# Block-wide loads of q, k and v, the weights issued together behind the first block, and the first attention as one chain

## The chip, the cores and the metric

The kernel runs on one core of one Trainium2 chip. The metric is the device time of one execution in microseconds (us); lower is better. TensorE is called PE, VectorE DVE, ScalarE ACT, GpSimd POOL and SyncE SP. SP does nothing here but issue transfers. The stage numbers below count position blocks of 128 from 0 to 5, and batches from 0 to 3.

## The reference

A decaying linear attention (4 batches, 8 heads, 768 positions, head size 64, all fp32) is followed by a two-layer network with a leaky activation on 3072 tokens of width 512:

```python
for b in range(nb):                      # blocks of 64 positions
    intra = einsum('bhic,bhjc->bhij', qb, kb) * Dmask     # lam ** (i - j), lower triangle
    intra = einsum('bhij,bhjd->bhid', intra, vb)
    inter = einsum('bhid,bhde->bhie', qb * lam_pow, kv_state)
    out[:, :, sl] = intra + inter
    kv_state = lam_block * kv_state + einsum('bhsd,bhse->bhde', kb * rev_pow, vb)
x = out.transpose(0, 2, 1, 3).reshape(B * S, H * D)
h = x @ w_in                             # 512 -> 2048
g = maximum(h, 0) + alpha * minimum(h, 0)
return g @ w_out                         # 2048 -> 512
```

## The kernel before

The kernel uses blocks of 128 positions (`L`), six of them (`NSB`), instead of the reference's 64. For each block `sb` and each batch `b` the attention has these steps:

- `load` brings q, k and v, each as a tile of 128 positions by 512 values in fp32 (256 KB). In memory a head's row is 64 values, so every piece of a transfer is 256 bytes. SP issues the loads.
- `casts` turns them into fp16 (`q16`, `k16`, `v16`) and makes `kdec`, the decayed k, on POOL. A string such as "AGG" says which engine casts q, k and v (A is ACT, V is DVE, G is POOL).
- `transposes` turns q16 and k16 on PE and copies them out of PSUM into `qkT`; from block 1 on POOL also makes `qdT`, the decayed q.
- `scores` multiplies k by q on PE; DVE multiplies by `dmask` into `sm`.
- `outputs` adds the state's part (`R` with `qdT`, from block 1 on) and the block's own part (`v16` with `sm`) in the PSUM tile `ot`; ACT copies it into `xT`, which holds all four batches of one block.
- `states` updates `R` with the product of `kdec` and `v16`.

The network follows block by block. `up(c, f)` makes one of 16 slices of 128 hidden units for block `c`: four matmuls into `h_ps`, a Relu of the negative part on ACT (`m`), and one DVE instruction that adds it with the factor `oma` = 1 - alpha. The arguments `b0, nb` restrict it to some batches, so that it can start when half of `xT` is there. `down(c, t, part, nparts)` makes a part of the second product for one batch of the block, and `store` writes it.

The weights come in four quarters each (`load_win`, `load_wout`), issued by POOL, which casts them to fp16 on the way (1 MB read, 512 KB written). All transfers, whoever issues them, run on the same 16 DMA engines.

The order is written out by hand: each engine runs its instructions in the order of the program, and waits only for the data and the buffers that it needs. Lines 399 to 483 are this order for blocks 0 and 1; from line 484 on `weave` alternates the attention steps of a block with `down` and `up` calls, and PE takes them strictly in turn. Two `gate` transfers (2 bytes each) on SP's queue hold back the loads behind them until a quarter of a weight has landed: gate 0 reads a column of `w_in_sb` ahead of block 1's loads, gate 1 a row of `w_out_sb` ahead of block 2's.

With `raw_pool` of six buffers for each of q, k and v, one and a half blocks of loads can be in flight. The attention of block 2 starts with two batches at once:

```python
        steps = [
            lambda: (casts(sb, 0, "AGG"), casts(sb, 1, "AGG")),
            lambda: transposes(sb, 0, "V"),
            lambda: scores(sb, 0),
        ]
```

Of the kernel before, what the change touches and what calls it, by code (L numbers as in the profile page):

```python
# [11 lines left out]
def kernel(  # L12
# [11 lines left out]
    nc = tc.nc  # L24
    ctx.enter_context(tc.manual_schedule())
    fp32 = mybir.dt.float32
# [3 lines left out]
    ALU = mybir.AluOpType  # L30

    B, H, S, D = q.shape
    assert (B, H, S, D) == (4, 8, 768, 64)
    L = 128
    NSB = S // L
    NHP = H // 2
    DM = H * D
    DFF = moe_w_in.shape[1]
    NF = DFF // 128
# [1 line left out]
    CH = B * L  # L41

    const = ctx.enter_context(tc.tile_pool(name="const", bufs=1))
    raw_pool = ctx.enter_context(tc.tile_pool(name="raw", bufs=6))
    half_pool = ctx.enter_context(tc.tile_pool(name="half", bufs=3))
    qkt_pool = ctx.enter_context(tc.tile_pool(name="qkt", bufs=2))
    sm_pool = ctx.enter_context(tc.tile_pool(name="sm", bufs=2))
# [12 lines left out]
    )  # L60
    raws = {}

    def load(sb, b):
        raws[sb, b] = []
        for n, src in zip("qkv", (q, k, v)):
            t = raw_pool.tile([128, DM], fp32, tag=f"{n}raw", name=f"{n}raw")
            nc.sync.dma_start(  # L67
                out=t.rearrange("p (h d) -> p h d", h=H),
                in_=src[b, :, ds(sb * L, L), :].rearrange("h s d -> s h d"),
            )  # L70
            raws[sb, b].append(t)

    w_in_sb = const.tile([128, NHP, DFF], fp16, name="w_in_sb")
    w_out_sb = const.tile([128, NF, DM], fp16, name="w_out_sb")
# [1 line left out]
    def load_win(i):  # L76
        nc.gpsimd.dma_start(
            out=w_in_sb[:, :, ts(i, 512)],
            in_=moe_w_in[:, ts(i, 512)].rearrange("(g p) f -> p g f", p=128),
        )  # L80

    def load_wout(i):
        nc.gpsimd.dma_start(
            out=w_out_sb[:, ts(i, 4), :],
            in_=moe_w_out[ts(i, 512), :].rearrange("(f p) d -> p f d", p=128),
        )
# [3 lines left out]
    def gate(i, w):  # L90

        nc.sync.dma_start(out=gates[:, i : i + 1], in_=w)

    load(0, 0)
    alpha_sb = const.tile([128, NF], fp32, name="alpha_sb")
    load(0, 1)
    nc.sync.dma_start(out=alpha_sb, in_=moe_alpha.rearrange("(t p) -> p t", p=128))
    load(0, 2)
    load(0, 3)


    one = const.tile([128, 1], fp32, name="one")
# [2 lines left out]
    nc.scalar.activation(warm, one, AF.Ln)  # L105
    ident = const.tile([128, 128], fp16, name="ident")
    make_identity(nc, ident)

    rel_i = const.tile([128, L], int32, name="rel_i")
    nc.gpsimd.iota(rel_i, pattern=[[1, L]], base=0, channel_multiplier=-1)  # L110
# [17 lines left out]

    dmask = const.tile([128, 2, NHP, L], fp32, name="dmask")
    for hl in range(2):  # L130
        nc.vector.tensor_tensor(
            out=dmask[:, hl],
            in0=rel_f.unsqueeze(1).to_broadcast([128, NHP, L]),
            in1=llv[:, hl, :].unsqueeze(2).to_broadcast([128, NHP, L]),
            op=ALU.mult,
        )
        nc.scalar.activation(dmask[:, hl], dmask[:, hl], AF.Exp)
        nc.gpsimd.affine_select(
            out=dmask[:, hl],
            in_=dmask[:, hl],  # L140
            compare_op=ALU.is_ge,
            fill=0.0,
            base=0,
            pattern=[[0, NHP], [1, L]],
            channel_multiplier=-1,
        )
# [10 lines left out]
    def late_constants():  # L157
        nc.vector.tensor_tensor(
            out=qdecay,
            in0=pos_f.unsqueeze(1).to_broadcast([128, NHP, L]),  # L160
            in1=llp.unsqueeze(2).to_broadcast([128, NHP, L]),
            op=ALU.mult,
        )
        nc.scalar.activation(qdecay, qdecay, AF.Exp)
        nc.scalar.activation(rdecay, llp, AF.Exp, scale=float(L))
        nc.vector.tensor_scalar(
            out=oma, in0=alpha_sb, scalar1=-1.0, scalar2=1.0, op0=ALU.mult, op1=ALU.add
        )


# [12 lines left out]
            nc.gpsimd.tensor_copy(out=out, in_=in_)  # L183

    def casts(sb, b, eng):
        qr, kr, vr = raws.pop((sb, b))
        q16 = half_pool.tile([128, DM], fp16, tag="q16", name="q16")
        k16 = half_pool.tile([128, DM], fp16, tag="k16", name="k16")
        v16 = half_pool.tile([128, DM], fp16, tag="v16", name="v16")
        copy_on(eng[0], q16, qr)  # L190
        copy_on(eng[1], k16, kr)
        copy_on(eng[2], v16, vr)
        T[sb, b] = dict(q16=q16, k16=k16, v16=v16)
        if sb < NSB - 1:
            kdec = half_pool.tile([128, DM], fp16, tag="kdec", name="kdec")
            nc.gpsimd.tensor_tensor(  # L196
                out=kdec.rearrange("p (h d) -> p h d", h=H),
                in0=kr.rearrange("p (h d) -> p h d", h=H),
                in1=kdecay.unsqueeze(2).to_broadcast([128, H, D]),
                op=ALU.mult,  # L200
            )
            T[sb, b]["kdec"] = kdec
# [194 lines left out]


    casts(0, 0, "VVG")
    load_win(0)  # L400
    transposes(0, 0, "V")
    casts(0, 1, "AAG")
    load_win(1)
    scores(0, 0)
    transposes(0, 1, "V")
    outputs(0, 0)
    scores(0, 1)
    casts(0, 2, "AVG")
    load_win(2)
    states(0, 0)  # L410
    transposes(0, 2, "A")
    outputs(0, 1)
    late_constants()
    scores(0, 2)
    states(0, 1)
    up(0, 0, 0, 2)
    casts(0, 3, "AVG")
    load_win(3)
    up(0, 1, 0, 2)
    outputs(0, 2)  # L420
    up(0, 2, 0, 2)
    transposes(0, 3, "A")
    up(0, 3, 0, 2)
    scores(0, 3)
    states(0, 2)
    outputs(0, 3)
    states(0, 3)
    for f in range(4):
        up(0, f, 2, 2)


    gate(0, w_in_sb[0:1, 0, 1024:1025])
    for b in range(B):
        load(1, b)
    for f in range(4, 11):
        up(0, f)
    casts(1, 0, "AGG")
    transposes(1, 0, "A")
    up(0, 11)
    casts(1, 1, "AGG")  # L440
    scores(1, 0)
    up(0, 12)
    transposes(1, 1, "A")
    up(0, 13)
    outputs(1, 0)
    casts(1, 2, "AGG")
    scores(1, 1)
    up(0, 14)
    states(1, 0)
    load_wout(0)  # L450
    transposes(1, 2, "A")
    up(0, 15)
    outputs(1, 1)
    casts(1, 3, "AGG")
    load_wout(1)
    scores(1, 2)
    up(1, 0, 0, 2)
    up(1, 1, 0, 2)
    states(1, 1)
    transposes(1, 3, "A")  # L460
    up(1, 2, 0, 2)
    outputs(1, 2)
    up(1, 3, 0, 2)
    load_wout(2)
    load_wout(3)
    scores(1, 3)
    up(1, 4, 0, 2)
    up(1, 5, 0, 2)
    states(1, 2)
    up(1, 6, 0, 2)  # L470
    outputs(1, 3)
    up(1, 7, 0, 2)
    states(1, 3)
    for f in range(8):
        up(1, f, 2, 2)
    gate(1, w_out_sb[0:1, 8, 0:1])
    for b in range(B):
        load(2, b)
    for f in range(8, NF):
        up(1, f)  # L480

    for b in range(B):
        load(3, b)
    weave(attention_steps(2), [lambda x=x: down(0, x // 4, x % 4, 4) for x in range(16)])
    for c in range(2, NSB):
        att = []
        if c + 2 < NSB:
            for b in range(B):
                load(c + 2, b)
        if c + 1 < NSB:  # L490
            att = attention_steps(c + 1)
        moe = []
        for f in range(NF):
            moe.append(lambda f=f: up(c, f))
            moe.append(lambda f=f: down(c - 1, f // 4, f % 4, 4))
        weave(att, moe)
# [32 lines left out]
```

## Time and profile before

| what | value |
|---|---|
| median of 3 runs | 247.33 us (245.26 to 249.1) |
| the profiled execution | 246.46 us |
| its span, first to last instruction | 244.7 us |
| PE busy | 217.8 us, 89% of the span |
| DVE, ACT, POOL busy | 124.7, 112.4, 86.3 us |
| DMA, mean over the span | 121 GB/s |
| granted PE clock | 1.00 |

The profile is of one execution. "Busy" adds up the instructions of an engine, whether they lie on the path that sets the end or not; a wait is put down to the instruction or transfer that ended it. "Landing" is the time from the issue of a transfer to its completion as the waiting engine sees it. The time of the profiled execution is 1.76 us longer than its span, for what lies around the first and the last instruction.

### The profile page before, as it was taken

What the parts mean: (1) busy time and instruction counts of PE and PEld (TensorE: products, weight loads), DVE (VectorE), ACT (ScalarE), POOL (GpSimd) and SP (SyncE); (2) the same over time, 40 slices, a digit from 0 to 9 for tenths busy, and PEclk for the clock granted to TensorE, in tenths of its full rate; (3) what the DMA queues carried; (4) which work ended last, traced back from release to release, by engine and by line L of the source; (5) the groups of instructions that cost most, each with busy time, mean ns of one, the idle gap of its engine ahead of it and who ended that gap; (6) DMA issues with size and microseconds to landing.
All of it is one profiled execution on the core that took longest, in us unless ns stands there. A gap on an engine that the chain in (4) does not pass through costs nothing.

```text
span 244.7 us, 4422 instructions
## 1 busy us (share of the span) xinstructions
PE 217.8 (89%) x1728; PEld 110.9 (45%) x1728; DVE 124.7 (51%) x205; ACT 112.4 (46%) x200; POOL 86.3 (35%) x119
## 2 busy tenths in 40 slices
PE   0529597989997998999999999999999999999994
PEld 0316443556443444444444444444444444444453
DVE  3534476768862334566456565556565534444100
ACT  4427667856642324534434535435534443444211
POOL 1823317992058684515641614611330100000000
PEclk9999999999999999999999999999999999999999
DMA  6999699799999999999304901101101100111122
GB/s 140 153 218 196 101 229 218 130 133 183 187 203 246 248 226 260 197 255 220 96 2 119 228 3 43 43 3 43 43 3 43 46 24 20 43 43 46 43 86 86
DMA packets 84936, 29.65 MB, mean 121 GB/s; under 512 B 77620, under 2 KB 81972, under 8 KB 84916
## 3 DMA queue, kind: packets, MB, share of 16 engines
q1 hardware_dynamic: 76948, 18.89, 41.5%
q0 software_dynamic: 4224, 4.19, 11.3%
q10 hardware_dynamic: 3744, 6.30, 7.1%
q8 instruction: 13, 0.21, 0.4%
q14 instruction: 7, 0.06, 0.1%
HBM read 27.28 MB, written 6.29 MB: 137 GB/s over the span
## 4 chain that ended last, share of the span: by engine, by line
PE 67%; DMA 11%; POOL 8%; SPq 5%; ACT 3%; issue 3%; DVE 1%; ACTq 0%; POOLq 0%
PE o_ps L332 27%; PE h_ps L305 25%; DMA vraw<-in_v_dram 9%; PE o_ps L355 6%; SPq L67 5%; DMA w_in_sb<-in_moe_w_in_dram 2%; POOL kdec L196 2%; PE ot L245 2%; PE ot L255 2%; PE s L225 2%; POOL qdT L216 2%; POOL v L183 1%; ACT o_sb L345 1%; PE tp L210 1%; PE kv L283 1%
## 5 line engine op out<-in xcount | busy, mean ns | idle before, releaser
L317 DVE SCALAR_TENSOR_TENSOR g<-m,oma,h_ps 128x512 f16<-128x512 f32 (+1 forms) x108 | 73.6, 687 | 73.0 <-ACT m L314 71.4
L305 PE MATMUL h_ps<-xT,w_in_sb 128*128 128x512 f16 (+1 forms) x432 | 98.0, 359 | 2.8 <-ACT xT L265 1.8
L314 ACT ACTIVATE m<-h_ps 128x512 f32<-128x512 f32 (+1 forms) x108 | 59.4, 550 | 76.2 <-PE h_ps L305 75.4
L332 PE MATMUL o_ps<-w_out_sb,g 128*128 128x512 f16 x320 | 82.2, 380 | 0.4 <-ACT o_sb L345 0.2
L305 PEld LDWEIGHTS <-w_in_sb 128*128 128x128 f16 x432 | 40.1, 99 | 39.3 <-issue 3.6
L216 POOL TENSOR_TENSOR qdT<-qkT,qdecay 128x512 f16<-128x512 f16 x20 | 23.2, 1164 | 67.0 <-DVE qkT L181 65.2
L332 PEld LDWEIGHTS <-g 128*128 128x128 f16 x320 | 28.8, 98 | 32.5 <-issue 0.8
L235 DVE TENSOR_TENSOR sm<-s,dmask 128x512 f16<-128x512 f32 x48 | 30.8, 684 | 12.9 <-PE s L225 12.9
L345 ACT ACTIVATE o_sb<-o_ps 128x512 f32<-128x512 f32 (+1 forms) x25 | 14.5, 580 | 26.6 <-PE o_ps L332 15.5
L208 PE MATMUL tp<-ident,k 128*128 128x128 f16 x96 | 10.0, 230 | 13.5 <-DVE k L181 12.0
L196 POOL TENSOR_TENSOR kdec<-kraw,kdecay 128x512 f16<-128x512 f32 x20 | 20.8, 1042 | 0.0
L265 ACT ACTIVATE xT<-ot 128x512 f16<-128x512 f32 x24 | 14.3, 597 | 13.9 <-PE ot L255 12.8
L183 POOL CAST v<-vraw 128x512 f16<-128x512 f32 x24 | 14.7, 614 | 14.3 <-DMA vraw<-in_v_dram 12.5
L183 POOL CAST k<-kraw 128x512 f16<-128x512 f32 x20 | 12.2, 611 | 18.1 <-DMA kraw<-in_k_dram 18.1
L208 PEld LDWEIGHTS <-k 128*128 128x128 f16 x96 | 7.2, 102 | 18.9 <-DVE k L181 12.1
L179 ACT ACTIVATE q<-qraw 128x512 f16<-128x512 f32 x23 | 14.0, 623 | 1.8 <-DMA qraw<-in_q_dram 1.8
L181 DVE COPY qkT<-tp 128x1024 f16<-128x1024 f16 x18 | 12.4, 690 | 4.5 <-PE tp L210 4.4
L355 PE MATMUL o_ps<-w_out_sb,g 128*128 128x512 f16 (+1 forms) x80 | 14.0, 336 | 0.0
L225 PE MATMUL s<-qkT 64*128 64x128 f16 x192 | 10.2, 229 | 2.5 <-ACT qkT L179 1.5
L255 PE MATMUL ot<-sm,v 128*64 128x128 f16 x192 | 10.8, 236 | 1.1 <-DVE sm L235 1.1
L210 PE MATMUL tp<-ident,q 128*128 128x128 f16 x96 | 10.1, 231 | 1.8 <-ACT q L179 1.6
L225 PEld LDWEIGHTS <-qkT 64*128 64x128 f16 x192 | 5.8, 98 | 11.2 <-issue 6.4
(44 smaller groups left out, 90.0 us busy)
## 6 DMA issues: line engine op xcount, KB each, us to landing
qraw<-in_q_dram SPq DMA_DIRECT2D x24, 256.0 KB, 5.2
kraw<-in_k_dram SPq DMA_DIRECT2D x24, 256.0 KB, 5.2
vraw<-in_v_dram SPq DMA_DIRECT2D x24, 256.0 KB, 5.1
out_dram<-o_sb ACTq DMA_DIRECT2D x23, 256.0 KB, 2.0
w_in_sb<-in_moe_w_in_dram POOLq DMA_DIRECT2D x4, 512.0 KB, 6.3
w_out_sb<-in_moe_w_out_dram POOLq DMA_DIRECT2D x4, 512.0 KB, 7.2
out_dram<-o_sb ACTq DMA_DIRECT2D x2, 128.0 KB, 1.7
lam_sb<-in_lam_dram ACTq DMA_DIRECT2D x1, 4.0 KB, 3.5
```

The source lines that it names most:

```text
L183: nc.gpsimd.tensor_copy(out=out, in_=in_)
L196: nc.gpsimd.tensor_tensor(out=kdec.rearrange("p (h d) -> p h d", h=H), in0=kr.rearrange("p (h d) -> p h d", h=H), in1=kdecay.unsqueeze(2). ...
L208: nc.tensor.transpose(tp[:, 1, hp, :], t["k16"][:, ts(hp, D2)], ident)
L216: nc.gpsimd.tensor_tensor(out=qdT, in0=qkT[:, 0], in1=qdecay, op=ALU.mult)
L225: nc.tensor.matmul(s[hl][:, hp, :], lhsT=t["qkT"][p, 1, hp, :], rhs=t["qkT"][p, 0, hp, :], start=True, stop=True,)
L235: nc.vector.tensor_tensor(out=sm, in0=s[hl], in1=dmask[:, hl], op=ALU.mult)
L305: nc.tensor.matmul(h_ps[:, 0:n], lhsT=w_in_sb[:, gi, ts(f, 128)], rhs=XT[c][:, gi, cols], start=(gi == 0), stop=(gi == NHP - 1),)
L314: nc.scalar.activation(m[:, 0:n], h_ps[:, 0:n], AF.Relu, scale=-1.0)
L317: nc.vector.scalar_tensor_tensor(out=G[c, f][:, cols], in0=m[:, 0:n], scalar=oma[:, f : f + 1], in1=h_ps[:, 0:n], op0=ALU.mult, op1=ALU.add,)
L332: nc.tensor.matmul(o_ps, lhsT=G[c, f][:, ts(t, 128)], rhs=w_out_sb[:, f, :], start=(f == 0), stop=(f == NF - 1),)
L345: nc.scalar.activation(o_sb[:, 0:n], o_ps[:, 0:n], AF.Copy)
L355: nc.tensor.matmul(o_ps[:, 0:n], lhsT=G[c, f][:, ts(t, 128)], rhs=w_out_sb[:, f, ts(x, n)], start=(f == 0), stop=(f == NF - 1),)
```

## The change

- A raw tile now holds all four batches of a block for one of q, k, v (1 MB), with two buffers instead of six of a quarter of that size. Block 0 is loaded as before, one batch at a time into its part of the tile; block 1 in two halves of two batches; blocks 2 to 5 with one transfer for each of q, k and v.
- Alpha is loaded as 16 rows of 128 values at the end of block 0's loads, and turned on PE into a PSUM tile that shares the buffer of `ot`; before, it came column-wise in the middle of these loads.
- The two multiplications of `dmask` move from DVE to POOL, and the two masks that follow on POOL stand behind both.
- All four quarters of w_in are issued by POOL behind the casts of batch 2 of block 0; before, one stood behind each batch's casts. Quarters 1 to 3 of w_out are issued together behind the casts of batch 3 of block 1.
- The attention of block 0 runs through without `up` calls between its steps; `late_constants` moves to its end. The `up` calls of block 0 then cover all four batches at once, eight of them ahead of block 1's first casts.
- Gate 0 reads a column of w_in's second quarter instead of its third. Gate 1 and block 2's loads keep their place in SP's queue.
- The halves of `up(1, 0)` to `up(1, 7)` for batches 2 and 3 stand behind `up(1, 8)` to `up(1, 15)`.

```diff
--- before.py
+++ after.py
@@ -41,7 +41,7 @@
     CH = B * L
 
     const = ctx.enter_context(tc.tile_pool(name="const", bufs=1))
-    raw_pool = ctx.enter_context(tc.tile_pool(name="raw", bufs=6))
+    raw_pool = ctx.enter_context(tc.tile_pool(name="raw", bufs=2))
     half_pool = ctx.enter_context(tc.tile_pool(name="half", bufs=3))
     qkt_pool = ctx.enter_context(tc.tile_pool(name="qkt", bufs=2))
     sm_pool = ctx.enter_context(tc.tile_pool(name="sm", bufs=2))
@@ -60,15 +60,16 @@
     )
     raws = {}
 
-    def load(sb, b):
-        raws[sb, b] = []
-        for n, src in zip("qkv", (q, k, v)):
-            t = raw_pool.tile([128, DM], fp32, tag=f"{n}raw", name=f"{n}raw")
+    def load(sb, b0=0, nb=B):
+        if b0 == 0:
+            raws[sb] = [
+                raw_pool.tile([128, B, DM], fp32, tag=f"{n}raw", name=f"{n}raw") for n in "qkv"
+            ]
+        for t, src in zip(raws[sb], (q, k, v)):
             nc.sync.dma_start(
-                out=t.rearrange("p (h d) -> p h d", h=H),
-                in_=src[b, :, ds(sb * L, L), :].rearrange("h s d -> s h d"),
+                out=t[:, ds(b0, nb), :].rearrange("p b (h d) -> p (b h) d", h=H),
+                in_=src[ds(b0, nb), :, ds(sb * L, L), :].rearrange("b h s d -> s (b h) d"),
             )
-            raws[sb, b].append(t)
 
     w_in_sb = const.tile([128, NHP, DFF], fp16, name="w_in_sb")
     w_out_sb = const.tile([128, NF, DM], fp16, name="w_out_sb")
@@ -91,12 +92,10 @@
 
         nc.sync.dma_start(out=gates[:, i : i + 1], in_=w)
 
-    load(0, 0)
-    alpha_sb = const.tile([128, NF], fp32, name="alpha_sb")
-    load(0, 1)
-    nc.sync.dma_start(out=alpha_sb, in_=moe_alpha.rearrange("(t p) -> p t", p=128))
-    load(0, 2)
-    load(0, 3)
+    for b in range(B):
+        load(0, b, 1)
+    alpha_t = const.tile([NF, 128], fp32, name="alpha_t")
+    nc.sync.dma_start(out=alpha_t, in_=moe_alpha.rearrange("(t p) -> t p", p=128))
 
 
     one = const.tile([128, 1], fp32, name="one")
@@ -105,6 +104,8 @@
     nc.scalar.activation(warm, one, AF.Ln)
     ident = const.tile([128, 128], fp16, name="ident")
     make_identity(nc, ident)
+    ident_f = const.tile([NF, NF], fp32, name="ident_f")
+    nc.vector.tensor_copy(out=ident_f, in_=ident[0:NF, 0:NF])
 
     rel_i = const.tile([128, L], int32, name="rel_i")
     nc.gpsimd.iota(rel_i, pattern=[[1, L]], base=0, channel_multiplier=-1)
@@ -128,13 +129,14 @@
 
     dmask = const.tile([128, 2, NHP, L], fp32, name="dmask")
     for hl in range(2):
-        nc.vector.tensor_tensor(
+        nc.gpsimd.tensor_tensor(
             out=dmask[:, hl],
             in0=rel_f.unsqueeze(1).to_broadcast([128, NHP, L]),
             in1=llv[:, hl, :].unsqueeze(2).to_broadcast([128, NHP, L]),
             op=ALU.mult,
         )
         nc.scalar.activation(dmask[:, hl], dmask[:, hl], AF.Exp)
+    for hl in range(2):
         nc.gpsimd.affine_select(
             out=dmask[:, hl],
             in_=dmask[:, hl],
@@ -163,8 +165,10 @@
         )
         nc.scalar.activation(qdecay, qdecay, AF.Exp)
         nc.scalar.activation(rdecay, llp, AF.Exp, scale=float(L))
+        al = ps.tile([128, NF], fp32, tag="ot", name="al")
+        nc.tensor.transpose(al, alpha_t, ident_f)
         nc.vector.tensor_scalar(
-            out=oma, in0=alpha_sb, scalar1=-1.0, scalar2=1.0, op0=ALU.mult, op1=ALU.add
+            out=oma, in0=al, scalar1=-1.0, scalar2=1.0, op0=ALU.mult, op1=ALU.add
         )
 
 
@@ -183,7 +187,7 @@
             nc.gpsimd.tensor_copy(out=out, in_=in_)
 
     def casts(sb, b, eng):
-        qr, kr, vr = raws.pop((sb, b))
+        qr, kr, vr = (t[:, b, :] for t in raws[sb])
         q16 = half_pool.tile([128, DM], fp16, tag="q16", name="q16")
         k16 = half_pool.tile([128, DM], fp16, tag="k16", name="k16")
         v16 = half_pool.tile([128, DM], fp16, tag="v16", name="v16")
@@ -397,96 +401,87 @@
 
 
     casts(0, 0, "VVG")
-    load_win(0)
     transposes(0, 0, "V")
     casts(0, 1, "AAG")
-    load_win(1)
     scores(0, 0)
     transposes(0, 1, "V")
     outputs(0, 0)
+    casts(0, 2, "AVG")
+    for i in range(4):
+        load_win(i)
     scores(0, 1)
-    casts(0, 2, "AVG")
-    load_win(2)
     states(0, 0)
     transposes(0, 2, "A")
     outputs(0, 1)
-    late_constants()
+    casts(0, 3, "AVG")
     scores(0, 2)
     states(0, 1)
-    up(0, 0, 0, 2)
-    casts(0, 3, "AVG")
-    load_win(3)
-    up(0, 1, 0, 2)
+    transposes(0, 3, "A")
     outputs(0, 2)
-    up(0, 2, 0, 2)
-    transposes(0, 3, "A")
-    up(0, 3, 0, 2)
     scores(0, 3)
     states(0, 2)
+    late_constants()
     outputs(0, 3)
     states(0, 3)
-    for f in range(4):
-        up(0, f, 2, 2)
-
-
-    gate(0, w_in_sb[0:1, 0, 1024:1025])
-    for b in range(B):
-        load(1, b)
-    for f in range(4, 11):
+
+
+    gate(0, w_in_sb[0:1, 0, 512:513])
+    load(1, 0, 2)
+    load(1, 2, 2)
+    for f in range(8):
         up(0, f)
     casts(1, 0, "AGG")
     transposes(1, 0, "A")
+    up(0, 8)
+    scores(1, 0)
+    up(0, 9)
+    casts(1, 1, "AGG")
+    up(0, 10)
+    outputs(1, 0)
     up(0, 11)
-    casts(1, 1, "AGG")
-    scores(1, 0)
+    transposes(1, 1, "A")
+    states(1, 0)
     up(0, 12)
-    transposes(1, 1, "A")
+    scores(1, 1)
+    casts(1, 2, "AGG")
     up(0, 13)
-    outputs(1, 0)
-    casts(1, 2, "AGG")
-    scores(1, 1)
+    load_wout(0)
     up(0, 14)
-    states(1, 0)
-    load_wout(0)
+    outputs(1, 1)
+    up(0, 15)
     transposes(1, 2, "A")
-    up(0, 15)
-    outputs(1, 1)
+    states(1, 1)
+    up(1, 0, 0, 2)
     casts(1, 3, "AGG")
-    load_wout(1)
+    for i in range(1, 4):
+        load_wout(i)
+    up(1, 1, 0, 2)
     scores(1, 2)
-    up(1, 0, 0, 2)
-    up(1, 1, 0, 2)
-    states(1, 1)
+    up(1, 2, 0, 2)
+    up(1, 3, 0, 2)
+    outputs(1, 2)
     transposes(1, 3, "A")
-    up(1, 2, 0, 2)
-    outputs(1, 2)
-    up(1, 3, 0, 2)
-    load_wout(2)
-    load_wout(3)
+    up(1, 4, 0, 2)
+    states(1, 2)
+    up(1, 5, 0, 2)
     scores(1, 3)
-    up(1, 4, 0, 2)
-    up(1, 5, 0, 2)
-    states(1, 2)
     up(1, 6, 0, 2)
+    up(1, 7, 0, 2)
     outputs(1, 3)
-    up(1, 7, 0, 2)
     states(1, 3)
+    for f in range(8, NF):
+        up(1, f)
+    gate(1, w_out_sb[0:1, 8, 0:1])
+    load(2)
     for f in range(8):
         up(1, f, 2, 2)
-    gate(1, w_out_sb[0:1, 8, 0:1])
-    for b in range(B):
-        load(2, b)
-    for f in range(8, NF):
-        up(1, f)
-
-    for b in range(B):
-        load(3, b)
+
+    load(3)
     weave(attention_steps(2), [lambda x=x: down(0, x // 4, x % 4, 4) for x in range(16)])
     for c in range(2, NSB):
         att = []
         if c + 2 < NSB:
-            for b in range(B):
-                load(c + 2, b)
+            load(c + 2)
         if c + 1 < NSB:
             att = attention_steps(c + 1)
         moe = []
```

## The prediction

> **What bounds the kernel now.** I first read the page for where TensorE idles.
>
> ```profile
> span 244.7 us, 4422 instructions
> PE 217.8 (89%) x1728; PEld 110.9 (45%) x1728; DVE 124.7 (51%) x205; ACT 112.4 (46%) x200; POOL 86.3 (35%) x119
> PE   0529597989997998999999999999999999999994
> ```
>
> Each digit is one slice of 6.1 us. Of the 26.9 us in which PE is idle, the table of stretches puts 21 us ahead of 75 us; from 80 us to the last output PE is busy over 97% of the time. So after about 75 us nothing can be won back: whatever the changed head loses by then stays in the time. The question is when PE passes the entry of the third position block, outputs(2, 0). Next the chain that ended last, in order of time, and the timeline around it:
>
> ```profile
> 64.73 1.31 SPq L67
> 66.10 6.08 DMA vraw<-in_v_dram
> 73.88 1.17 POOL qdT L216
> ```
>
> ```profile
> 61.25 0.60 SPq L92 DMA_DIRECT2D gates<-w_out_sb  x1
> 61.95 0.38 SPq L67 DMA_DIRECT2D qraw<-in_q_dram  x1
> ...
> 66.10 1.06 SPq L67 DMA_DIRECT2D vraw<-in_v_dram  x1
> ...
> 72.30 0.62 POOL L183 CAST v<-vraw 128x512 f16<-128x512 f32 x1 [1.64 <-DMA vraw<-in_v_dram]
> ...
> 75.09 0.41 PE L245 MATMUL ot<-qdT,R 64*64 64x128 f16 x8 [1.34 <-POOL qdT L216]
> ```
>
> The reader sees one path: the gate on w_out's third quarter passes at 61.25, load(2) is issued behind it, v of batch 1 lands at 72.2, POOL casts it, makes kdec and then qdT of batch 0 (casts of batches 0 and 1 are queued ahead of that qdT), and PE, after 1.34 us of waiting, starts outputs(2, 0) at 75.09. Block 2's entry is already a DMA wait; it is short because six 256 KB transfers suffice.
>
> What releases the gate is in the waits of the SP queue and in POOL's timeline:
>
> ```profile
> SPq L92 <- DMA w_out_sb<-in_moe_w_out_dram: 17.9, 1, 17.9
> ```
>
> ```profile
> 35.38 0.60 POOL L183 CAST k<-kraw 128x512 f16<-128x512 f32 x1 [7.34 <-DMA kraw<-in_k_dram]
> 36.59 0.62 POOL L183 CAST v<-vraw 128x512 f16<-128x512 f32 x1 [0.60 <-DMA vraw<-in_v_dram]
> ...
> 50.14 1.03 POOL L196 TENSOR_TENSOR kdec<-kraw,kdecay 128x512 f16<-128x512 f32 x1
> 51.13 0.81 POOL L83 DMA_DIRECT2D w_out_sb<-in_moe_w_out_dram  x1
> ...
> 53.64 1.55 POOL L83 DMA_DIRECT2D w_out_sb<-in_moe_w_out_dram  x2
> ```
>
> POOL works almost without a gap from 37 to 56 us, so the w_out issues come when POOL is through block 1's casts, and those begin when load(1)'s first batch lands. The sum follows this path.
>
> **The head.** *Alpha.* Column-wise it is 2048 four-byte elements. SP's next issue behind it, at 8.10, is held 2.29 us, and DMA traffic falls to nothing between 9.7 and 11.2 us; q of batch 2 lands 2.3 us behind v of batch 1 where neighbours are 1.2 us apart. By rows (16 pieces of 512 B, last in line) that goes. In the undisturbed stretch a 256 KB transfer lands every 1.2 us, so with v(0, 1) at 10.7 as now, v(0, 2) lands at 10.7 + 3 x 1.2 = 14.3 instead of 20.1 and v(0, 3) at 18.0 instead of 25.5.
>
> *dmask on POOL.* Two multiplies leave DVE (1.29 us for both). POOL's nearest rows for 512 elements are kdec (1.04) and qdT (1.16), a third f32 row, rd with 256, is 0.61; bounds 0.7 to 1.3, I take 1.1. The masks end at about 8.4 instead of 8.2, and DVE casts q and k 0.6 us sooner. Neither decides: transposes(0, 1) waits for k(0, 1), which lands at 9.6 either way. The extra copy on DVE is like the 0.17 us copies. The PE transpose of alpha has no f32 row; the f16 one is 0.23, bounds 0.03 to 1; it and oma share the ot buffer, so outputs(0, 3) waits for them, up to some 1 us. All of this is covered by the wait for load(1) below; uncovered it would cost about 1.
>
> *w_in behind the cast.* POOL now issues all four quarters after v16 and kdec of batch 2: 14.4 + 0.6 + 1.03 = 16.05, then 0.81 each. Queued behind them on POOL are v16 and kdec of batch 3 (from 19.3); PE waits for those little. Landing 6 us after issue and then one per 3.3 us (w_out's quarters land so, 58.0, 61.2, 63.7), they arrive near 22, 25.3, 28.6 and, shared, 33.5, where now they land at 16.2, 21.0, 27.8 and 32.8. Attention(0) as one chain ends near 24, and up(0, 0) to up(0, 7) run to about 32.5 (eight at 0.86 us, the first two at half speed as at 20.97).
>
> *Gate 0 and load(1).* The gate now waits for the second quarter: 25.3 instead of 27.8. But the first load is two batches wide, so casts(1, 0) need six 256 KB units instead of three. From traffic at about 28 us, some 5.5 us pass beside w_in, at 2.4 us per unit (the pace between 11.5 and 18 us, with w_in beside), then 1.2 us each: 2.3 units by 33.7, four (k) by 36, six (v) by 38.4. Now v lands at 36.4. PE is through its eight ups at 32.5 and waits in transposes(1, 0) until 36.7: a **new stall of about 4 us**, behind it in PE's order all of block 1.
>
> **POOL to the second gate.** From v(1, 0) to the end of casts(1, 3), POOL has four times v16 and kdec (1.6), three times k16 (0.55), three qdT (1.15), two rd (0.6) and w_out's first quarter (0.8): about 13.5 us, and 2 us of waiting for PE and ACT between batches (2.3 us now). 38.4 + 15.3 = 53.7, where kdec of (1, 3) now ends at 51.17. Quarters 1 to 3 of w_out then go out back to back: the third lands 5.5 us after the second's issue plus 3.3 us: **62.5** instead of 61.2. Issuing them together earns about 1.2 us back.
>
> **Load(2), the main term.** Casts(2, 0) now need q, k and v of all four batches: three 1 MB transfers, each with one completion. Today's twelve transfers of load(2), the same bytes with the same 256 B elements, end with v(2, 3), issued at 73.95 and landing in 5.6: 79.55, that is 18.3 us behind the gate. So v lands at 62.5 + 18.3 = 80.8, k about 12.9 behind the gate, 75.4. PE has done its ups and two downs by about 71 and waits for transposes(2, 0); behind it are all downs. POOL then needs v16 and kdec (1.6), k16, v16 and kdec of batch 1 (2.1) and qdT (1.17): outputs(2, 0) starts at 80.8 + 4.8 = **85.6, 10.5 us behind 75.09**.
> No row here shows a 1 MB load. Bounds: 291 GB/s, the best stretch of the head (about 4.2 to 4.9 us), gives 3.15 MB / 0.291 + 3.0 (the fastest landing of one transfer, at 61.95) = 13.8 behind the gate, 4.5 us less; the slowest pace, beside w_in, for one extra unit 1.2 more. I take 18.3, the row with the same neighbours.
>
> The Trainium skill speaks for the change here: "DMA: Bandwidth & Descriptors", section on measured HBM to SBUF transfers, says to batch transfers to 1 MiB or more, and its fit is 2.0 us plus bytes at 436 GB/s. As an estimate by that page v would land 9.2 us behind the gate and the sum would be near 249. The trace has many transfers in flight at once and 172 GB/s over these 18.3 us, so its own pace counts.
>
> **Cold matmuls.** After the idle stretch from 14 to 17.9 us, eight 256-wide matmuls take 1.89 us; at 48.02 eight take 1.03. All PE work between 17.9 and 23.7 is slow in this way, at most 2.3 us lost. PE waits twice near block 2's entry (71 to 75, 79.5 to 85.6); the first slowdown falls into the second wait. For the second I take 0.8 between 0 and 2.3, since POOL's qdT and casts pace the next steps.
> The skill's "TensorE: Matmul & The Clock Gate", Part 1, gives half clock after about 3.4 us of idleness and for about 3.4 us of work; as an estimate that is 1.7 instead of 0.8. The granted clock in the rows stays 1.00 throughout, so only the durations show it here.
>
> **Later blocks.** Load(3) follows at once (free buffer) and ends near 96, ahead of its use near 102; loads 4 and 5 wait for the casts of the same buffer two blocks before and have a stage of 36 us. Nothing.
>
> **Sum.** 10.5 + 0.8 = 11.3 on the span of 244.7, plus the 1.76 us around it (the profiled run's time is 246.46): 257.8. The median of the runs, 247.33, is 0.9 above that run and their spread is 3.8, so 2% is about what can be told from no change.
>
> **Rivals.** *Wide loads stream fast* (the other side). Place: load(2), and load(1) with it. For: 291 GB/s was reached, fewer completions. Against: in the long stretch from 64 to 80 us, with the queue always full, the traffic stays near 220 to 260 at best. Price: v 4.5 us sooner, load(1) 1.5 sooner, cold 0.5: 257.8 - 6.8 = 251. It decides from about 290 GB/s; to be faster by 2% the load would have to end 2 us behind the gate, which needs more than any stretch shows. Chance 0.09.
> *w_in starves load(1).* If the weights take more than half while both run, v(1, 0) lands at 41 to 42 and everything moves by 3 to 4: 261.5. For: between 11.5 and 18 us w_in's packets took 65.8% of the 16 engines' time and the loads' 51.8% (they overlap). Against: the bytes moved there were the same, 0.69 and 0.71 MB. Chance 0.14.
> *The first block isn't alone*: if the casts of batch 0 waited for the whole tile, they would start at 18 instead of 5, and the time would be near 269. Against: the ups at 20.97 read w_in's tile while its third quarter, issued ahead of them in program order, lands at 27.8. Chance 0.04.
> The forecast, 257.8, has 0.73; its own range is 253 to 261.5.
>
> **Numbers.** Range 252 to 262.5: the forecast's bounds, most of the starved case, and the edge of the fast one. Faster by over 2% 0.03 (no mechanism found, only an error in the whole path), same 0.08, slower 0.89.
>
> **What would show it.** Right: kraw of block 1 waited for by PE for about 4 us near 33 to 37; the second gate near 62; 1 MB loads landing with v near 81; PE idle twice between 71 and 86; outputs(2, 0) near 85.6; from there the same spacing as now. Wrong: block 2's entry at or before 80, a second gate before 58, or load(2) through within 14 us.

## The result and the profile after

The changed kernel takes 261.73 us in the median of 4 runs (260.83 to 263.11), against 247.49 us for the kernel before (245.26 to 249.1). The ratio is 1.061, with a 95% interval of 1.052 to 1.070: it is slower by 14.2 us. The forecast was 257.8, so the direction was right and the loss was larger than expected: 14.2 us instead of 10.3. The profiled execution took 260.83 us, with a span of 258.9 us.

The first lines are from the page of the changed kernel: the span, PE in 40 slices (now 6.5 us each), and the granted PE clock in tenths.

```profile
span 258.9 us, 4309 instructions
PE   0676859766984899899999999999999999999994
PEclk9999979998899599999999999999999999999999
```

PE is busier in the first slices than before. But it has dips from the sixth slice (32 us) to the thirteenth (84 us), and the clock row, which held nines throughout before the change, falls in or just behind some of them. From the fourteenth slice on PE is at eight tenths or more up to the last slice, as before the change.

The next lines are from the timeline of the changed kernel, along the path that the prediction followed (start, duration, engine, line, what; idle time and its cause in brackets).

```profile
35.37 0.40 PE L212 MATMUL tp<-ident,k 128*128 128x128 f16 x4 [3.91 <-POOL k L187]
37.12 0.62 POOL L187 CAST v<-vraw 128x512 f16<-128x512 f32 x1 [1.80 <-DMA vraw<-in_v_dram]
...
53.80 1.03 POOL L200 TENSOR_TENSOR kdec<-kraw,kdecay 128x512 f16<-128x512 f32 x1
54.78 2.30 POOL L84 DMA_DIRECT2D w_out_sb<-in_moe_w_out_dram  x3
...
64.39 0.62 SPq L93 DMA_DIRECT2D gates<-w_out_sb  x1
...
75.36 1.89 PE L336 MATMUL o_ps<-w_out_sb,g 128*128 128x512 f16 x8
78.89 0.40 PE L212 MATMUL tp<-ident,k 128*128 128x128 f16 x4 [1.64 <-POOL k L187]
...
83.10 0.62 POOL L187 CAST v<-vraw 128x512 f16<-128x512 f32 x1 [4.27 <-DMA vraw<-in_v_dram]
85.33 0.61 PE L212 MATMUL tp<-ident,k 128*128 128x128 f16 x4 [3.66 <-POOL k L187]
...
88.01 0.63 PE L249 MATMUL ot<-qdT,R 64*64 64x128 f16 x8
```

Each step can be read off. Block 1's first k comes late and PE waits 3.91 us. POOL is through block 1's casts at 54.8. The second gate passes at 64.39. Then v of block 2, a whole 1 MB, is there 18.7 us behind the gate, and outputs(2, 0), the entry of block 2, starts at 88.01 where it started at 75.09 before. That is 12.9 us. From this entry to the end of the span 170.9 us pass (258.9 - 88.01), against 169.6 before (244.7 - 75.09); the missing 1.3 us lie in the rows just behind the entry, where matmuls run at half speed.

Here is the same subtraction for every kernel of this case. "Gate 1" is the passing of the second gate, "entry" the start of outputs(2, 0) in the profiled execution, "rest" is its span minus the entry, "median" the time of the runs. The labels are those of the experiments below.

| kernel | gate 1 | entry | rest | median |
|---|---|---|---|---|
| before | 61.25 | 75.09 | 169.6 | 247.49 |
| after | 64.39 | 88.01 | 170.9 | 261.73 |
| l2_halves | 63.90 | 79.59 | 169.6 | 251.60 |
| l2_batches | 64.21 | 79.94 | 169.8 | 251.58 |
| no_gate1 | none | 79.24 | 169.9 | 251.44 |
| l1_batches | 61.47 | 85.28 | 171.2 | 257.35 |
| before_wide | 61.77 | 86.50 | 169.9 | 257.91 |
| fill | 63.45 | 87.17 | 169.6 | 259.27 |
| no_gate1_l1 | none | 77.20 | 169.5 | 248.68 |
| rd_early | none | 72.94 | 169.5 | 244.32 |
| rd_early_up | none | 73.47 | 169.8 | 244.98 |
| after_rd | 61.85 | 85.73 | 169.9 | 257.40 |
| before_rd | 61.45 | 75.08 | 169.6 | 246.87 |
| before_rows | 62.43 | 76.30 | 169.6 | 247.31 |

From the entry on, the kernels agree to 0.4 us (169.5 to 169.9), with 1 MB loads or with 256 KB ones. The two exceptions, the changed kernel and l1_batches, show a low granted clock just behind the entry (0.50 and 0.69 from 85 to 90 us). So 12.9 us of the change lie ahead of block 2's entry and 1.3 us just behind it.

### The profile page after: what moved, and what is told of

It is laid out like the page before. It is cut to its first block, busy times and chain, and to the rows that moved or that the text cites. A ratio compares the mean times of both kernels' runs of the same rounds, so it can differ in the third digit from the quotient of the medians.

```text
span 258.9 us, 4309 instructions
## 1 busy us (share of the span) xinstructions
PE 225.2 (87%) x1713; PEld 112.5 (43%) x1713; DVE 124.8 (48%) x200; ACT 111.8 (43%) x196; POOL 88.2 (34%) x121
## 3 DMA queue, kind: packets, MB, share of 16 engines
q1 hardware_dynamic: 37380, 18.88, 37.0%
## 4 chain that ended last, share of the span: by engine, by line
PE 64%; DMA 13%; SPq 7%; POOL 5%; ACT 4%; issue 3%; DVE 3%; ACTq 0%; POOLq 0%; DVEq 0%
PE o_ps L336 26%; PE h_ps L309 23%; DMA vraw<-in_v_dram 9%; SPq L69 6%; PE o_ps L359 5%; DMA w_in_sb<-in_moe_w_in_dram 3%; PE ot L259 3%; PE ot L249 2%; PE s L229 2%; POOL kdec L200 2%; DVE sm L239 1%; PE tp L214 1%; POOL qdT L220 1%; ACT o_sb L349 1%; DVE g L321 1%
## 5 line engine op out<-in xcount | busy, mean ns | idle before, releaser
L321 DVE SCALAR_TENSOR_TENSOR g<-m,oma,h_ps 128x512 f16<-128x512 f32 (+1 forms) x104 | 72.7, 706 | 81.0 <-ACT m L318 79.6
L309 PE MATMUL h_ps<-xT,w_in_sb 128*128 128x512 f16 (+1 forms) x416 | 100.4, 375 | 4.2 <-DVE g L321 2.2
L318 ACT ACTIVATE m<-h_ps 128x512 f32<-128x512 f32 (+1 forms) x104 | 58.5, 564 | 81.6 <-PE h_ps L309 80.9
L336 PE MATMUL o_ps<-w_out_sb,g 128*128 128x512 f16 x320 | 83.7, 385 | 0.5 <-ACT o_sb L349 0.5
L309 PEld LDWEIGHTS <-w_in_sb 128*128 128x128 f16 x416 | 39.3, 100 | 44.6 <-issue 9.8
L212 PEld LDWEIGHTS <-k 128*128 128x128 f16 x96 | 7.3, 105 | 23.6 <-POOL k L187 10.7
L259 PE MATMUL ot<-sm,v 128*64 128x128 f16 x192 | 12.2, 242 | 5.4 <-DVE sm L239 3.9
L259 PEld LDWEIGHTS <-v 128*64 128x64 f16 x192 | 7.7, 118 | 8.5 <-issue 6.5
L214 PE MATMUL tp<-ident,q 128*128 128x128 f16 x96 | 10.7, 241 | 0.8 <-ACT q L183 0.6
## 6 DMA issues: line engine op xcount, KB each, us to landing
out_dram<-o_sb ACTq DMA_DIRECT2D x23, 256.0 KB, 2.0
qraw<-in_q_dram SPq DMA_DIRECT2D x4, 256.0 KB, 5.2
kraw<-in_k_dram SPq DMA_DIRECT2D x4, 256.0 KB, 5.1
vraw<-in_v_dram SPq DMA_DIRECT2D x4, 256.0 KB, 5.1
```

Of the source, the lines that this page charges most:

```text
L212: nc.tensor.transpose(tp[:, 1, hp, :], t["k16"][:, ts(hp, D2)], ident)
L259: nc.tensor.matmul(ot[ds(hl * 64, 64), hp, :], lhsT=t["v16"][:, ds((2 * hp + hl) * D, D)], rhs=t["sm"][hl][:, hp, :], start=(sb == 0 and h ...
L309: nc.tensor.matmul(h_ps[:, 0:n], lhsT=w_in_sb[:, gi, ts(f, 128)], rhs=XT[c][:, gi, cols], start=(gi == 0), stop=(gi == NHP - 1),)
L318: nc.scalar.activation(m[:, 0:n], h_ps[:, 0:n], AF.Relu, scale=-1.0)
L321: nc.vector.scalar_tensor_tensor(out=G[c, f][:, cols], in0=m[:, 0:n], scalar=oma[:, f : f + 1], in1=h_ps[:, 0:n], op0=ALU.mult, op1=ALU.add,)
L336: nc.tensor.matmul(o_ps, lhsT=G[c, f][:, ts(t, 128)], rhs=w_out_sb[:, f, :], start=(f == 0), stop=(f == NF - 1),)
```

## Experiments

The theory is the prediction's: block 2's entry waits for whole 1 MB loads behind a gate that itself comes late. The rivals are that a wide transfer is slow by itself, that PE is late by its own work in blocks 0 and 1, and that cold matmuls make the loss.

**Narrower loads for block 2.** Two kernels change only the loads of block 2.

```diff
 # l2_halves
-    load(2)
+    load(2, 0, 2)
+    load(2, 2, 2)
 # l2_batches
-    load(2)
+    for b in range(B):
+        load(2, b, 1)
```

> The changed kernel, but block 2's q, k and v come in two transfers of two batches each instead of one of four. Theory (the wait for whole 1 MB loads sets block 2's entry): casts of batches 0 and 1 need half the bytes, so v lands about 11 to 14 us behind the second gate instead of 18.7; PE is then held by its own work (two downs at 75.4 and 6 us of steps behind them), outputs(2, 0) starts near 81.5 instead of 88.0, and the time falls by 6.5 to 8 us to about 254. Rival (PE is late by itself, from cold matmuls and the order of block 1, and the load only fills that time): the time stays above 259.

> The changed kernel, but block 2's loads go batch by batch in twelve transfers of 256 KB, as before the change. Theory: the same as with halves, since batches 0 and 1 are cast together either way: outputs(2, 0) near 81.5, about 254. If the size of a transfer itself made the wait (a slow pace of wide transfers), this one would be clearly faster than halves, by 2 us or more.

Measured: 251.60 us for halves and 251.58 for batches (ratios to before 1.020, 1.017 to 1.024, and 1.019, 1.017 to 1.022). Both win 10.1 us, more than expected, and they are equal. The timeline of the kernel with halves shows v of batches 0 and 1 where it showed 83.10 above:

```profile
73.45 1.89 PE L336 MATMUL o_ps<-w_out_sb,g 128*128 128x512 f16 x8
74.19 0.62 POOL L187 CAST v<-vraw 128x512 f16<-128x512 f32 x1 [1.86 <-DMA vraw<-in_v_dram]
...
79.59 0.41 PE L249 MATMUL ot<-qdT,R 64*64 64x128 f16 x8
```

The gate passed at 63.90, so v landed 10.3 us behind it. The entry no longer waits for anything (no bracket): PE is held by its own order, two downs at 73.45 and the steps behind them. PE starts these downs 5.9 us later than in the kernel before (67.55); in the changed kernel the load's wait covers that. What was waited for was the other batches' bytes, not the size of a transfer: with batch-wise transfers v of batch 0 is cast at 70.84 and nothing is gained by it, since the casts of batches 0 and 1 come as a pair and PE isn't there yet.

**No second gate.** The 1 MB loads stay, but they follow block 1's loads at once.

```diff
-    gate(1, w_out_sb[0:1, 8, 0:1])
     load(2)
```

> The changed kernel without the second gate: block 2's 1 MB loads follow block 1's loads at once. Theory: v of block 2 lands near 60, long before its use, so the width costs nothing; block 2's entry is then PE's own, outputs(2, 0) near 81.5, about 254. Rival (the weights suffer): w_out's quarters share the DMA engines with the loads of blocks 2 and 3, the first downs wait for the fourth quarter, and the time stays above 257.

Measured: 251.44 us (1.021, 1.017 to 1.025).

```profile
60.39 0.62 POOL L187 CAST v<-vraw 128x512 f16<-128x512 f32 x1 [0.75 <-DMA vraw<-in_v_dram]
...
79.24 0.41 PE L249 MATMUL ot<-qdT,R 64*64 64x128 f16 x8
```

The width costs nothing when the load has time: POOL casts v of block 2 at 60.39, and the entry, 79.24, is PE's own, as with halves. The starved weights did not show: the downs at 73.11 waited for no quarter of w_out. Three ways to take the load off the path end within 0.2 us of each other, so this wait is worth 10.1 to 10.3 us of the 14.2.

**The width alone, in the kernel before.** Tiles for four batches with two buffers, and from block 2 on one transfer for each of q, k and v; nothing else.

```diff
-    for b in range(B):
-        load(2, b)
+    load(2)
...
-    for b in range(B):
-        load(3, b)
+    load(3)
```

> The kernel before, with one edit: blocks 2 to 5 load q, k and v with one 1 MB transfer each (and tiles for all four batches, two buffers); order, gates, weights, alpha and blocks 0 and 1 as before. Theory (whole-block loads behind the second gate are the main loss by themselves): the gate stays near 61.3, v lands 18.7 later at 80, POOL needs 4.9, so outputs(2, 0) starts near 85 instead of 75.1; with 1.3 for cold matmuls the time is near 257.5. Rival (the loss needs block 1's late arrival too): below 252.

Measured: 257.91 us (1.042, 1.036 to 1.048), 10 us over the kernel before. In its timeline PE is through its first two downs at 69.6, as early as ever, and then stands:

```profile
67.72 1.89 PE L333 MATMUL o_ps<-w_out_sb,g 128*128 128x512 f16 x8
76.87 0.61 PE L209 MATMUL tp<-ident,k 128*128 128x128 f16 x4 [7.26 <-POOL k L184]
...
86.50 0.41 PE L246 MATMUL ot<-qdT,R 64*64 64x128 f16 x8 [1.19 <-POOL qdT L217]
```

The gate was at 61.77, as before, and the entry came 24.7 us behind it. So one edit of the change makes 10 of the 14 us even with everything else undone, and the same 10 us are won by undoing it for block 2. The rest of the change costs some 4 us in both cases, in different ways. With the load's wait it is 3.8 us on the medians (261.73 - 257.91) and 2.5 between the profiled spans: the gate comes 2.6 us later, the entry follows it 1.1 us sooner, and 1.0 us more is lost behind the entry. Without the wait it is 4.1 us (251.6 - 247.5), and there PE itself comes late to the entry.

**Block 1's loads batch by batch.** First alone, then without the second gate.

```diff
-    load(1, 0, 2)
-    load(1, 2, 2)
+    for b in range(B):
+        load(1, b, 1)
```

> The changed kernel, but block 1's loads go batch by batch. Theory: k and v of batch 0 land near 32 and 33.5 instead of 34.6 and 37.0, PE's wait at 31.5 to 35.4 nearly goes, POOL's chain and with it the second gate come some 3 us sooner (near 61.5), and as that gate still holds the wide loads, outputs(2, 0) starts near 85 and the time is about 258.5. Rival (POOL's chain through block 1 is paced by waits for PE and DVE, not by its start): the gate moves by less than 1 us and the time by less than 1.

> The changed kernel without the second gate and with block 1's loads batch by batch. Theory: with neither wait for wide loads left, block 1 starts 3 us sooner than without the gate alone (251.4), the first downs come near 69.5, and the time is 247.5 to 248.5, the kernel before's. Rival (block 1's new order holds PE whatever the loads do): it stays above 250.

Measured: 257.35 us alone (1.042, 1.039 to 1.046), a little better than expected, and 248.68 without the gate (1.005, 1.002 to 1.009). Alone, these are the two ends of the path:

```profile
33.50 0.40 PE L212 MATMUL tp<-ident,k 128*128 128x128 f16 x4 [1.30 <-POOL k L187]
...
85.28 0.64 PE L249 MATMUL ot<-qdT,R 64*64 64x128 f16 x8
```

PE's wait ahead of transposes(1, 0) falls from 3.91 to 1.30 us, v is cast at 33.89 instead of 37.12, the gate passes at 61.47 (2.9 us sooner) and the entry comes 23.8 us behind it: the chain POOL, gate, wide load holds. Without the gate the halves for block 1 cost 2.8 us (251.44 - 248.68), all ahead of the entry (79.24 against 77.20). What is left over the kernel before is 1.2 us; the edits behind it (`dmask` on POOL, the order of the weights and of the `up` calls) were not run one by one.

**Matmuls that keep PE busy.** Fourteen 512-column matmuls on weights that are there, into a PSUM buffer that nobody reads, in each of the two long waits; they add work and leave out nothing.

```diff
+    fill(14)
     transposes(1, 0, "A")
...
+                if sb == 2 and b == 0:
+                    steps.append(lambda: fill(14))
                 steps.append(lambda b=b: transposes(sb, b + 1, "V"))
```

> The changed kernel with 14 matmuls of 512 columns without a use put into each of PE's two long waits: ahead of transposes(1, 0) (wait of 3.9 us) and of transposes(2, 1) (3.7 us). Their 3.0 us lie in the waits. Theory (PE runs at half speed after a long wait): the granted clock stays 1.00 at 35 to 40 and 85 to 90 us, the steps from outputs(2, 0) on at 88.0 lose 1.3 us less, and block 1 is up to 1 us sooner: the time falls by 1.3 to 2.3 to about 260. Rival (the low clock costs nothing there since POOL paces these steps): the time stays within 0.5.

Measured: 259.27 us (1.047, 1.042 to 1.053), 2.5 us less than the changed kernel. The table by stretches (start and end, length, busy time of PE, PEld, DVE, ACT, POOL, then the granted clock, the DMA share and GB/s) first for the changed kernel:

```profile
35.00:40.00 5.00, 4.63 (x27) 2.01 (x27) 1.53 (x3) 1.86 (x3) 3.20 (x5) 0.66 1.34 217
85.00:90.00 5.00, 4.67 (x31) 2.39 (x32) 0.69 (x1) 0.75 (x2) 5.00 (x7) 0.50 1.09 258
```

and for the kernel with the added matmuls:

```profile
35.00:40.00 5.00, 4.74 (x41) 2.31 (x39) 2.01 (x4) 2.59 (x5) 3.25 (x5) 1.00 1.24 218
85.00:90.00 5.00, 3.89 (x40) 1.77 (x37) 1.44 (x3) 1.12 (x2) 5.00 (x6) 1.00 0.98 234
```

In these stretches the clock stays at 1.00, the rest falls from 170.9 to 169.6, and the gate comes 0.9 us sooner. So the low clock is part of the loss, 1.3 us behind the entry and about 0.8 ahead of it (88.01 to 87.17), and filling these two waits takes it away.

**Alpha alone.** The kernel before with alpha by rows at its old place.

```diff
-    alpha_sb = const.tile([128, NF], fp32, name="alpha_sb")
-    nc.sync.dma_start(out=alpha_sb, in_=moe_alpha.rearrange("(t p) -> p t", p=128))
+    alpha_t = const.tile([NF, 128], fp32, name="alpha_t")
+    nc.sync.dma_start(out=alpha_t, in_=moe_alpha.rearrange("(t p) -> t p", p=128))
...
+        nc.tensor.transpose(al, alpha_t, ident_f)
```

> The kernel before with alpha loaded as 16 rows at its old place in SP's queue and turned on PE. Theory: the stretch without DMA traffic near 9.7 to 11.2 us goes, q of batch 2 of block 0 lands at 12 instead of 13.4, and as block 1's loads still wait for the gate on w_in's third quarter, which POOL issues behind batch 2's casts, the gate comes 1 to 2 us sooner; of that 0 to 1.5 us reach the end: 245.5 to 247. Rival: alpha's elements cost nothing on the path, the time is the same within 0.5.

Measured: 247.31 us, ratio 1.000 (0.996 to 1.005). The stretch from 10 to 12 us now moves 207 GB/s instead of 88, gate 0 passes at 26.04 instead of 27.80, and v of block 1 is cast at 34.47 instead of 36.59. In the profiled run (247.68 us) none of it arrives: PE's up calls at 28.5 are slow (44 matmuls in 10.08 us, before 8.23), transposes(1, 0) starts at 38.41 instead of 36.83, and POOL then waits 5.23 us for qkT. The ten runs spread from 246.15 to 249.57, and only this one was read. The rival is right on the time; the bubble itself was real.

**The order of POOL in block 1.** In the changed kernel the waits put this line among the larger ones of DVE:

```profile
DVE R L298 <- POOL rd L277: 5.2, 4, 2.0
```

`rd`, the decayed state, needs nothing of block 1, but stands behind each batch's qdT in POOL's order. Three kernels make block 1's four `rd` ahead of gate 0, where POOL is idle. The first two are built on no_gate1_l1, the second with one more `up` ahead of block 1's casts and block 2's ungated loads in halves; the third is the changed kernel with only this edit, and a fourth is the kernel before with it.

```diff
+    early_rd()                # rd1[:, b] = R[b] * rdecay on POOL, for all b
     gate(0, w_in_sb[0:1, 0, 512:513])
...
-        if sb > 0:
+        if sb == 1:
+            rd = rd1[:, b]
+        elif sb > 1:
             rd = sm_pool.tile([128, NHP, D], fp32, tag="rd", name="rd")
```

> The kernel without the second gate and with block 1's loads batch by batch (248.7), and POOL makes block 1's four decayed states (rd) ahead of gate 0, in its idle time between 21 and 32 us, instead of behind each qdT. Theory (in block 1 DVE's state update waits for POOL's rd, 5.0 us in three waits, and holds DVE's other work and with it PE): these waits go, the last xT of block 1 is ready 2 to 4 us sooner than 59.6, and the time falls by 2 to 3.5 us to about 246, at or below the kernel before. Rival (POOL's qdT or PE's own work paces block 1): the time stays within 0.7 of 248.7.

> The same, with one more up call of block 0 ahead of block 1's first casts (PE waits 1.15 us there) and block 2's ungated loads in two halves. Theory: PE's wait at 32.3 us goes and v of block 2 lands some 4 us before 67.8, so nothing of the loads is left on the path: 0.5 to 1.5 us below the other kernel of this call. Rival: no difference over 0.5.

> The changed kernel with nothing but the early rd: gate 1 and all wide loads stay. Theory (block 2's entry hangs on POOL's chain to w_out's third quarter and on the wide load behind it): POOL's chain is 1 to 2 us shorter up to the w_out issues, the gate passes near 62.5 to 63.5 instead of 64.4, outputs(2, 0) follows 23 to 24 us behind it as now, and the time falls by 1 to 2 us only, where the same edit without the gate won 4.4. Rival (PE's lateness in block 1 decides here too): a fall of 4 us or more.

> The kernel before with nothing but the early rd (POOL is idle from 28 to 35 us, and works without a gap from 39 to 56). Theory: POOL's chain through block 1 is up to 2.4 us shorter, w_out and gate 1 with it, and PE ends block 1 that much sooner: 245 to 246. Rival (the order of the steps on PE and ACT paces block 1 in this kernel): within 0.7 of the kernel before.

Measured: rd_early 244.32 us, ratio 0.987 (0.983 to 0.990): faster than both kernels, and 4.4 us below no_gate1_l1, more than the 2 to 3.5 expected. rd_early_up 244.98, ratio 0.990 (0.986 to 0.993), no better, so its two further edits bring nothing. after_rd 257.40 (1.042, 1.038 to 1.047). before_rd 246.87 (0.997, 0.994 to 1.001), no difference, as the rival said: POOL's first wait for qkT grows from 1.53 to 3.23 us, gate 1 passes at 61.45, and the entry is at 75.08.

after_rd fell by 4.3 us in the medians, 3.3 between the two profiled spans, and not by the 1 to 2 of the theory; on the number alone the rival won. The timeline says otherwise: the gate passes at 61.85, 2.5 us sooner, the entry at 85.73 follows 23.9 us behind it as it did (23.6), and PE's first downs, 6.2 us sooner at 69.12, only lead to a longer wait:

```profile
69.12 1.89 PE L349 MATMUL o_ps<-w_out_sb,g 128*128 128x512 f16 x8
76.62 0.61 PE L212 MATMUL tp<-ident,k 128*128 128x128 f16 x4 [5.61 <-POOL k L187]
```

The remaining 1.0 us goes with a clock of 0.91 instead of 0.50 at 85 to 90 us. So the chain decides there; how much the edit shortens it was underestimated.

## Why the mechanism held, and the step of the prediction that failed

**What held.** The bound (block 2's entry; nothing is won back behind it) is shown by the column "rest". The chain from load(1) over POOL's casts, w_out's third quarter and the second gate to the 1 MB loads is shown by l1_batches, after_rd and before_wide, in which the entry follows the gate by 23.8 to 24.7 us (23.6 in the changed kernel) wherever that lies. Load(2), the main term, was put at 18.3 us behind the gate and took 18.7; POOL's steps behind it were put at 4.8 and took 4.9. Wide transfers of later blocks were put at nothing, and cost nothing (169.6 behind the entry in fill, as before the change). The rival of fast wide loads (13.8 us behind the gate) is out, and so is the one in which block 0's first casts wait for the whole tile: q and k of batch 0 were cast by 7.7 us.

**What was too small.** On the span the sum gave 256.0 and the profile 258.9. These 2.9 us are three terms:

- *POOL to the second gate*, the step that failed: forecast 62.5, measured 64.39, 1.9 us.
- *Load(2) and POOL's steps behind it*: 0.4 and 0.1 us.
- *Cold matmuls* behind the entry: 0.8 set, 1.3 measured by the column "rest", and fill takes just this away.

The step that failed has three parts. First, v of block 1 came at 37.1, 1.3 us sooner than forecast: gate 0 passed at 24.73 instead of 25.3, and the loads then took 0.7 us less than the row beside w_in suggested. Second, from there to the end of casts(1, 3) POOL took 17.7 us instead of 15.3, and all of this is waiting. The forecast set 2 us for POOL's waits, near the 2.3 that it had read in the kernel before; they were 4.4 us, both for qkT:

```profile
43.88 1.16 POOL L220 TENSOR_TENSOR qdT<-qkT,qdecay 128x512 f16<-128x512 f16 x1 [1.90 <-ACT qkT L183]
...
50.98 1.15 POOL L220 TENSOR_TENSOR qdT<-qkT,qdecay 128x512 f16<-128x512 f16 x1 [2.50 <-ACT qkT L183]
```

About 0.6 us of the first wait goes with the low clock behind PE's stall: in fill, l2_halves and no_gate1, where the clock stayed at 1.00 from 35 to 40 us, this wait is 1.28 or 1.29 us. The forecast had the stall of 4 us, but put the slow matmuls behind it at nothing in block 1; fill gets the gate 0.9 us sooner. The rest of the two waits is there in every kernel that has this order of block 1 and `rd` at its old place (1.3 to 2.0 and 2.5 us). After_rd has 1.69 and 1.69 us in spite of a low clock, and its casts end 2.5 us sooner, 1.2 us of it from `rd`'s own work. What else in the new order makes these waits no run shows. Third, w_out's third quarter landed 9.6 us behind the end of these casts (9.4 to 9.8 in the other kernels with this order and the gate), and the sum had 8.8.

The last 0.9 us to the median is the scatter between the profiled execution and the others (260.83 and 261.73); the sum was made against one execution of the kernel before, which also lay 0.9 under its median, and I hadn't added that. The measured median lies inside the stated range, 252 to 262.5, and just above the forecast's own, 253 to 261.5.

Some figures in the prediction do not come out of its own rows. 13.5 and 2 us are 15.5, not 15.3, and at its own paces v of block 1 lands at 38.1, not 38.4, so the two slips nearly cancel. The waits given as 2.3 us for the kernel before are 1.53 and 0.25 us in POOL's timeline. The price of fast wide loads adds up to 6.5 us, not 6.8.

**What was right by luck.** The sum let the head's loss vanish under the wait for load(2), with PE through two downs at 71. PE was through them at 77.25 (75.36 + 1.89), 7.8 us later than before the change: a low clock and block 1's waits for DVE came on top of the one stall that was foreseen. It stayed covered, because k of block 2 was cast only at 78.22 and PE still waited 1.64 us for it. The three kernels without the load's wait show what lay under it: they end at 251.4 to 251.6, some 4 us over the kernel before, and the forecast had no term for that. The rival in which w_in starves load(1) was priced at 261.5, next to the measured 261.73. That is chance too: its sign, v of block 1 at 41 to 42, did not come (37.1).

**The skill's two rules.** Twelve transfers of load(2) ended 18.3 us behind the gate and three of 1 MB 18.7. The Trainium skill, "DMA: Bandwidth & Descriptors", section on measured transfers, recommends 1 MiB or more, and its figures are for transfers that GpSimd issues. With SP issuing and the queue always full, this case shows nothing of that gain, and the later completion is what counted.

The granted clock fell to 0.66 and 0.50 behind waits of 3.9 and 3.7 us, and stayed at 1.00 behind those of 1.30 (l1_batches) and 1.34 us (the kernel before). "TensorE: Matmul & The Clock Gate", Part 1, puts the limit near 3.4 us of idleness; these four rows agree. But the length of one wait doesn't sort all rows of this case. The first line is of after_rd, the second of l2_halves, both at transposes(1, 0):

```profile
34.95 0.61 PE L212 MATMUL tp<-ident,k 128*128 128x128 f16 x4 [2.33 <-POOL k L187]
```

```profile
35.35 0.40 PE L212 MATMUL tp<-ident,k 128*128 128x128 f16 x4 [2.86 <-POOL k L187]
```

Behind the shorter wait the clock was 0.50 from 35 to 38 us, behind the longer one it stayed at 1.00. In the changed kernel it was also 0.50 from 64 to 66 us, where no wait since 50 us was over 1.72 us, but PE had been busy for only 1.8 of the 4 us from 58 to 62. The 36 matmuls from 62.24 on took 9.19 us instead of 7.50 (l2_halves); this lay under the load's wait.

## What to carry to other kernels

A transfer is waited for as a whole: v of block 2's first batches could be cast 18.7 us behind the gate with one transfer, and 10.3 us behind it with halves. Widen loads only where a whole stage lies between issue and use, and count the bytes ahead of the first consumer, not the number of transfers. When a long wait is found, price what lies under it as well, by a run in which that wait is taken away; here 10 of 14 us went with it, and PE's late start, which the wait had covered, kept the other 4. An instruction that needs nothing of its batch (`rd`) can be issued ahead of the batch's work, in the engine's idle time, but what that gains depends on what paces the path: the same edit won 4.4 us in one order of these steps and none in the other.

## What the runs showed of the hardware

The packets of SP's queue fell from 76,948 to 37,380 for the same 18.9 MB. Halves for block 2 alone bring 9,264 of them back (46,644), about three quarters of the 12,288 pieces of 256 B that a block has; so by these counts a transfer of four batches goes in packets of 1 KB, and one of two batches does not. The queue's share of the DMA engines' time fell too, from 41.5% of 244.7 us to 37.0% of 258.9, 101.6 to 95.8 us, though before_rd, with the loads of the kernel before, has 98.9. But the bytes did not land sooner in the stretch that mattered.

```profile
q1 hardware_dynamic: 76948, 18.89, 41.5%
```

```profile
q1 hardware_dynamic: 37380, 18.88, 37.0%
```

The first line is of the kernel before, the second of the changed one (queue, packets, MB, share of 16 engines).

Alpha's 2048 four-byte elements kept SP's next issue for 2.29 us, and the DMA engines ran almost empty behind them (88 GB/s from 10 to 12 us). With 16 rows instead, in before_rows, the same issue took 0.42 us, and the stretch moved 207 GB/s:

```profile
8.10 2.29 SPq L67 DMA_DIRECT2D qraw<-in_q_dram  x1
```

```profile
7.88 0.42 SPq L67 DMA_DIRECT2D qraw<-in_q_dram  x1
```
